# Inner sums of x ahead of the sixth out product's additions in VectorE's order (last two units of a RetNet + SwiGLU kernel)

## The chip, the cores and the metric

The kernel runs on one core of a Trainium2 chip. The core's engines are TensorE (PE in the profile, PEld for its weight loads), VectorE (DVE), ScalarE (ACT), GpSimd (POOL) and SyncE (SP, which issues the DMAs). The metric is the device time of one execution in microseconds; lower is better.

## The reference, cut to what matters

The program computes a retention layer and then a gated feed-forward network, all in float32:

```python
scores = q @ k^T / 8                      # (8 batches, 8 heads, 576, 576), head dimension 64
x = (scores * decay) @ v                  # -> x of 4608 tokens x 512
xn = x / sqrt(mean(x * x) + 1e-6) * rms_g
g, val = xn @ w_gate, xn @ w_val          # 512 -> 1536 each
out = (g * sigmoid(g) * val) @ w_out      # 1536 -> 512
```

The change lies in the second part, between the end of one block of tokens and the start of the next.

## The kernel before, in words

**Units.** The 4608 tokens are worked in nine units of 512 (u = 0 to 8). x of a unit is held transposed, as four chunks of 128 features by 512 tokens. Units 0 and 1 and the retention of the early batches are worked in a written-out plan; the loop at the end of the program does u = 2 to 8. Each pass of it has an up phase (`up` or `up_deep`, six pieces n = 0 to 5, which alternate between gate and value) and an out phase (`across`).

**Fewer products.** Both phases use a 2 x 2 block scheme of seven products in place of eight (Strassen's, in Winograd's form), which needs sums and differences of the blocks before the products and additions of the products behind them. In the out phase and in the deep stages the scheme is applied twice, one inside the other: seven outer products of seven inner ones. The blocks are called A11, A12, S1, A22, S2, S3, S4.

**Deep stages.** For the last two units (LATE: u = 7 and 8) the first four up pieces (DEEP: n = 0 to 3) are done by `up_deep`. Each has seven outer products in the order A11, S2, S1, S3, A12, S4, A22; each outer product is seven inner ones (line 884, 128 x 128 by 128 x 128, two matmul instructions each, 14 in all), which write two PSUM banks: xo and xp, then yo and yp, zo and zp, wo and wp, then xo/xp, zo/zp and wo/wp again. VectorE adds them up (line 905) and ScalarE copies some (line 901). GpSimd then combines the results (line 913), and ScalarE (gate, SiLU, line 925) or VectorE (value, product, line 923) makes h of them one stage later.

**The moving operands of a deep stage.** Three of the seven inner products of an outer product take a plain quarter of an operand; the other four need inner sums. `inner_x` (lines 837 to 857) makes them ahead of the unit, once for all four stages, in two parts:

- part 0 fills the tile inner_x from x itself, for the blocks A11, S1, A12 and S4: four additions of 128 x 512;
- part 1 fills the tile deep_x (deep_x2 in the code) from the tile sums, for the blocks S2, S3 and A22: four additions of 128 x 384.

In each part the first two additions are independent of each other; the third needs the second, and the fourth the third. The first deep product (A11) needs part 0 alone. The second (S2) needs part 1: first its three plain inner products are worked (yo twice, yp once), then the four with deep_x.

**The out phase.** `across(u)` is a generator. It makes its operands and then works seven outer products n = 0 to 6 (line 1090) into the banks of x, z, x, z, y, w, x. Each product has an early and a late half, and the generator yields after each half, so that the caller can put other work between them: yield 0 comes before the first product, yield 2n + 1 after the early half of product n and yield 2n + 2 after its late half and the additions that follow it. What follows the last three products is:

- n = 4 (banks yo, yp): two additions each into two of the four blocks of vec (the tile vi), and one addition of 128 x 896 (line 1113);
- n = 5 (banks wo, wp), the sixth product: `add(3, 3, "w")` and `add(1, 1, "w")`, four VectorE operations (line 1117: wo 128 x 512 and wp 128 x 384, each twice);
- n = 6 (banks xo, xp), the seventh: `add(1, 1, "x")`, two operations.

Behind them GpSimd combines vec (`combine`, line 1286). GpSimd also makes the inner sums of the out operands ahead of their products (lines 1042 and 1047).

**Between the two.** The loop behind `across(u)` puts the preparation of unit u + 1 at yields of `across(u)`: its norm at yield 2, the scaling of x at 3 to 6, the sums of x (the tile sums, line 626) at 8, and, where u + 1 is 7 or 8, `inner_x` at the yields that the table XI_AT names: part 0 at yield 11, part 1 at yield 12.

**What sets the order.** The whole program is under `tc.manual_schedule()`: each engine works its instructions in the order in which the code issues them, and waits on semaphores where data or a buffer is not ready. So VectorE's order around the end of `across(u)` is: additions of n = 4, part 0, the four additions of n = 5, part 1, the two additions of n = 6, then the additions of the first deep stage.

**PSUM banks.** All of PSUM is one pool of eight banks; a new tile gets a bank that an earlier one has left. In units 7 and 8 the program places the first deep stage's banks so: x on those that the out phase's y left, y on those of z, z (zo, zp) on those of w (wo, wp), and w on those of x. So the third deep product, z, can write only when `add(1, 1, "w")` has read the banks of the sixth out product.

**Weights.** They stream from DRAM into one large tile (ring) by SyncE's DMAs, each issued when TensorE has used the piece whose place it takes.

Of the kernel before, what the change touches and what calls it, by code (L numbers as in the profile page):

```python
# [44 lines left out]
def kernel(  # L45
# [11 lines left out]
    nc = tc.nc  # L57
# [200 lines left out]
    def prepare(j):  # L258

        d = st[j]  # L260
        for odd in range(2):
            t = d["qraw"][:, odd::2]
            nc.scalar.activation(
                out=t, in_=t, func=AF.Copy, scale=gp[:, jobs[j][1], odd : odd + 1]
            )
        for nm in ("q", "k"):
            t = att.tile([P, S], F32, tag=nm + "T", name=f"{nm}T_{j}")
            nc.vector.transpose(out=t, in_=d.pop(nm + "raw").rearrange("p t a -> p (t a)"))
            d[nm + "T"] = t
        scale_v(j)  # L270
# [364 lines left out]
    LATE = (NU - 2, NU - 1)  # L635
# [172 lines left out]
    def inner_blocks(u, n):  # L808


        i = pieces.index(("up", u, n))
        assert n_used <= i < n_sent
        a, z = places[i]
        w = ring[:, a:z].rearrange("p (b x) -> p b x", b=7)
        d = w_in_d[n - DEEP[0]]
        t6 = vi[:, NV : NV + 6 * 4 * P].rearrange("p (b s f) -> p b s f", b=6, s=4)
        t1_ = row(f"inner_{n}").rearrange("p (b s f) -> p b s f", b=1, s=4)
        for t, b in ((t6, slice(0, 6)), (t1_, slice(6, 7))):
            a11, a21, a12, a22 = (w[:, b, i * P : i * P + P] for i in range(4))
            s1, s2, s3, s4 = (t[:, :, i] for i in range(4))  # L820
            for o, x, y, op in (
                (s3, a11, a21, ALU.subtract), (s1, a21, a22, ALU.add),
                (s2, s1, a11, ALU.subtract), (s4, a12, s2, ALU.subtract),
            ):
                nc.gpsimd.tensor_tensor(out=o, in0=x, in1=y, op=op)

        def save(i):
            b = PLACE[IN_ORDER[i]]
            t = t6[:, b] if b < 6 else t1_[:, 0]
            nc.sync.dma_start(  # L830
                out=d[:, i * 4 * P : i * 4 * P + 4 * P], in_=t.rearrange("p s f -> p (s f)")
            )

        saves.extend(lambda i=i: save(i) for i in range(7))

    def inner_x(u, part, eng):


        if not deep_x1:
            retention.close()  # L840
            late = ctx.enter_context(tc.tile_pool(name="late", bufs=1))
            deep_c.extend(late.tile([P, 4, 7, P], F32, name=f"deep_c_{i}") for i in range(2))
            deep_x2.append(late.tile([P, 4, 3, P], F32, name="deep_x2"))
            deep_x1.append(
                xp.tile([P, NHP, U], F32, tag="x", name="inner_x")
                .rearrange("p k (a t h) -> p k a t h", a=2, t=2)
            )
        x = x_of[u].rearrange("p (a c) (t s h) -> p c s a t h", c=2, t=2, s=2)
        y = sums_x.rearrange("p i c (s h) -> p c s i h", s=2)
        for o, v_ in (((deep_x1[0], x), (deep_x2[0], y))[part],):  # L850
            t1_, t3, t2, t4 = (o[:, i] for i in range(4))
            x11, x12, x21, x22 = v_[:, 0, 0], v_[:, 0, 1], v_[:, 1, 0], v_[:, 1, 1]
            for r, a, b, op in (
                (t1_, x12, x11, ALU.subtract), (t3, x22, x12, ALU.subtract),
                (t2, t3, x11, ALU.add), (t4, x21, t2, ALU.subtract),
            ):
                eng.tensor_tensor(out=r, in0=a, in1=b, op=op)  # L857

    def up_deep(u, n):

# [174 lines left out]
    def inner_sums(u, n, part=None, eng=nc.gpsimd):  # L1035

        x = operands_of(u)[order_of(u)[n]]
        x11, x12 = x[:, :NK, :P], x[:, :NK, P:]
        x21, x22 = x[:, NK:, :P], x[:, NK:, P:]
        i1, i3, i2, i4 = inner_of(u, n)  # L1040
        if part != 1:
            eng.tensor_tensor(out=i1, in0=x12, in1=x11, op=ALU.subtract)  # L1042
        c = slice(1, NK) if part == 1 else slice(0, 1) if part == 0 else slice(0, NK)
        for o, a, b, op in (
            (i3, x22, x12, ALU.subtract), (i2, i3, x11, ALU.add), (i4, x21, i2, ALU.subtract),
        ):
            eng.tensor_tensor(out=o[:, c], in0=a[:, c], in1=b[:, c], op=op)  # L1047
# [231 lines left out]
    def combine(b, eng=nc.vector, late=False):  # L1279

        t = vec[:, b] if isinstance(b, slice) else vec[:, b : b + 1]
        for o, x, y in (
            (A12, A11, A12), (A11, A11, S2), (S1, A11, S1), (S4, S1, S4), (A11, A11, S3),
            (S3, S1, S3), (A22, A11, A22),
        ):
            eng.tensor_tensor(out=t[:, :, o], in0=t[:, :, x], in1=t[:, :, y], op=ALU.add)  # L1286
        if late:
            store(NU - 1, b)
# [3 lines left out]
    def store(u, b=None):  # L1292

        rows = out[u * U : u * U + U].rearrange("(C c p) (R r x) -> c r p C R x", C=2, c=2, R=2, r=2)
        v4 = vec.rearrange("p (C R) n d -> p C R n d", C=2)
        for n, (r, c) in CORNERS.items():
            if b is None:
                for half in range(2):
                    nc.sync.dma_start(out=rows[c][r][:, half], in_=v4[:, half, :, n])
            else:  # L1300
                nc.sync.dma_start(out=rows[c][r][:, b // 2, b % 2], in_=vec[:, b, n])
# [252 lines left out]


    z = DEEP[-1]
    XI_AT = {11: (0, nc.vector), 12: (1, nc.vector)}
    FINISH = {(z + 1, 5): 1, (z + 1, 6): 1, (z + 2, 1): 1} if z % 2 else {(z + 1, 1): 3, (z + 1, 4): 2}
    with tc.manual_schedule():
        start()  # L1560
        for u in range(2, NU):
            j0 = NHP * (u + 1)
            more = u + 1 < B
            for n in range(2 * NG):
                deep = u in LATE and n in DEEP
                for i, _ in enumerate((up_deep if deep else up)(u, n)):
                    if u in MAKES:
                        if (n, i) == ((0, 0) if MAKES[u] < 4 else (1, 3)):
                            inner_blocks(u, MAKES[u])
                        if (n, i) == (0, 0):  # L1570
                            combine(slice(0, 4), nc.gpsimd)
                    if saves and (n, i) >= (0, 4):
                        saves.pop(0)()
                    if (n, i) == ((2 * NG - 1, 0) if u in MAKES else (1 + (u in LATE), 4)):
                        store(u - 1)
                    if (n, i) == ((2 * NG - 1, 2) if u in LATE else (2 * NG - 2, 1)):
                        inner_sums(u, 0, 0)
                        inner_sums(u, 1, 0)
                    if more and i == 2 and 0 < n <= NHP:
                        if j0 + n < len(jobs):  # L1580
                            prepare(j0 + n)
                            fetch(j0 + n + 1)
                    if u + 1 < NU and n == 2 * NG - 1:
                        if i < NHP:
                            gather(u + 1, i, square(u + 1, i))
                        elif i == NHP:
                            fold(u + 1)
                        elif i == 6:
                            meet(u + 1)
                    if (u, n, i) == (2, 2, 1):  # L1590
                        same_rows()
                    for _ in range(FINISH.get((n, i), 0) if u in LATE else 0):
                        unfinished.pop(0)()
                    if more and (n, i) == (NHP, 5) and j0 + NHP == len(jobs):
                        values(j0 + NHP - 1)
                if more and n <= NHP and (n or u == 2):
                    if j0 + n < len(jobs):
                        slot(j0 + n, rest=(n > 0))
                    else:
                        carried(j0 + n - 1)  # L1600
            assert not unfinished and not saves
            for i, _ in enumerate(across(u)):
                if u + 1 == NU:
                    continue
                if i == 2:
                    root(u + 1)
                elif i in (3, 4, 5, 6):
                    scale_x(u + 1, (i - 3,))
                elif i == 8:
                    sums_of_x(u + 1)  # L1610
                if i in XI_AT and u + 1 in LATE:
                    inner_x(u + 1, *XI_AT[i])


# [25 lines left out]
```

## Time and profile before

| | |
|---|---|
| timed runs | median 1093.52 us of 3 (1093.32 to 1093.53) |
| profiled execution | 1092.14 us, of which the span of the profile is 1090.3 us |
| TensorE busy | 1076.3 us, 99% of the span |
| VectorE busy | 763.6 us, 70% |
| GpSimd busy | 556.5 us, 51% |
| ScalarE busy | 337.0 us, 31% |
| granted TensorE clock | 0.998 of full speed |
| operations of part 1 (128 x 384) | 0.55 to 0.56 us each |
| operations of part 0 (128 x 512) | 0.69 us, three of eight 1.48 us |
| additions of the sixth product (line 1117) | 0.68 us (wo) and 0.55 us (wp) |

The times of single instructions come from the profiled execution, which is taken once; the median comes from runs without a profile. A stretch of the program is found in the timeline by its lines and tiles: the out phase of unit 6 ends and unit 7 begins at about 881 us, the out phase of unit 7 ends and unit 8 begins at about 983 us. Operations on one engine overlap at their edges: an operation can start before the one ahead of it has ended.

### The profile page before, as it was taken

To read this page: it belongs to the slowest core of one execution; us is meant where nothing else is said; L and a number is where in the kernel's file an instruction comes from. 1 tells how busy PE (TensorE), PEld (TensorE's weight loads), DVE (VectorE), ACT (ScalarE), POOL (GpSimd) and SP (SyncE) were. 2 spreads that over 40 slices of the span, in tenths; PEclk is the share of its full clock that TensorE was granted. 3 is DMA by queue.
4 is the path that set the end of the run, shared out by engine and by line. 5 is a ranking of instruction groups with operands and counts; after the bars stand their busy time and mean duration, and the time that the engine had idled before them with its cause. 6 is when DMAs were issued, how large, how long until landed. Compare 5 with 4: busy or idle time off the path is not lost. (4 is left out here: it accounts for less than half of the span.)

```text
span 1090.3 us, 25380 instructions
## 1 busy us (share of the span) xinstructions
PE 1076.3 (99%) x10342; PEld 913.9 (84%) x10342; DVE 763.6 (70%) x1355; ACT 337.0 (31%) x763; POOL 556.5 (51%) x509
## 2 busy tenths in 40 slices
PE   8899999999999999999999999999999999999998
PEld 6754444479988899889988998889888999899998
DVE  3878568877876775667667765777465877686677
ACT  5855564331123411332034202331233112212210
POOL 0026326538530288126652476229601968896876
PEclk9999999999999999999999999999999999999999
DMA  8856798697978976898779975889676889499951
GB/s 205 195 174 243 290 244 211 213 336 196 286 284 227 197 275 237 225 231 269 271 223 209 275 288 186 248 207 366 220 195 207 274 288 342 177 308 351 331 204 40
DMA packets 271860, 265.68 MB, mean 244 GB/s; under 512 B 194304, under 2 KB 214912, under 8 KB 266624
## 3 DMA queue, kind: packets, MB, share of 16 engines
q1 hardware_dynamic: 270304, 263.67, 77.7%
q8 instruction: 81, 1.33, 0.5%
q10 hardware_dynamic: 1440, 0.40, 0.2%
q14 instruction: 35, 0.29, 0.1%
HBM read 226.61 MB, written 37.42 MB: 242 GB/s over the span
## 5 line engine op out<-in xcount | busy, mean ns | idle before, releaser
L980 PE MATMUL up<-x,ring 128*128 128x512 f32 x384 | 167.1, 594 | 0.0
L980 PEld LDWEIGHTS up<-x,ring 128*128 128x128 f32 x384 | 72.2, 190 | 89.3 <-issue 84.9
L746 PE MATMUL x<-x,ring 128*128 128x256 f32 x544 | 130.8, 383 | 0.0
L746 PE MATMUL w<-sums,ring 128*128 128x256 f32 x544 | 128.6, 379 | 0.0
L746 PE MATMUL z<-x,ring 128*128 128x256 f32 x544 | 128.5, 379 | 0.0
L1042 POOL TENSOR_TENSOR vi<-h 128x384 f32<-128x384 f32 x32 | 41.7, 1304 | 161.4 <-DVE h L765 148.9
L746 PEld LDWEIGHTS z<-x,ring 128*128 128x128 f32 x544 | 103.4, 190 | 14.1
L746 PEld LDWEIGHTS w<-sums,ring 128*128 128x128 f32 x544 | 103.2, 190 | 14.2
L746 PEld LDWEIGHTS x<-x,ring 128*128 128x128 f32 x544 | 101.0, 190 | 14.2 <-ACT m L772 0.2
L1047 POOL TENSOR_TENSOR vi<-h 128x384 f32<-128x384 f32 (+2 forms) x46 | 45.6, 991 | 116.6 <-DVE h L765 116.6
L1286 POOL TENSOR_TENSOR vi<-vi 128x512 f32<-128x512 f32 (+1 forms) x77 | 79.5, 1045 | 36.3 <-DVE vi L1117 19.8
L913 POOL TENSOR_TENSOR deep_c<-deep_c 128x512 f32<-128x512 f32 x56 | 73.1, 1317 | 11.4 <-DVE deep_c L905 5.1
L746 PE MATMUL y<-sums,ring 128*128 128x256 f32 x272 | 64.3, 379 | 0.0
L753 DVE TENSOR_TENSOR h<-u,w 128x512 f32<-128x512 f32 x34 | 23.4, 687 | 49.8 <-PE w L746 49.8
L746 PEld LDWEIGHTS y<-sums,ring 128*128 128x128 f32 x272 | 51.7, 190 | 7.0
L1406 POOL TENSOR_TENSOR vi<-vi 128x512 f32<-128x512 f32 (+1 forms) x24 | 40.7, 1696 | 30.3 <-DVE vi L1395 16.9
L1406 POOL TENSOR_TENSOR ring<-ring 128x512 f32<-128x512 f32 x24 | 30.4, 1272 | 49.7 <-DMA w_up_blocks<-ring 24.8
L753 DVE TENSOR_TENSOR u<-m,y 128x512 f32<-128x512 f32 x34 | 23.3, 685 | 44.0 <-PE y L746 37.7
L767 ACT ACTIVATE h<-h 128x512 f32<-128x512 f32 x51 | 32.0, 629 | 62.6 <-DVE h L753 62.6
L334 DVE SCALAR_TENSOR_TENSOR ret<-s,causal 128x256 f32<-128x256 f32 (+2 forms) x112 | 32.0, 337 | 21.8 <-PE s L296 21.8
L1047 POOL TENSOR_TENSOR vi<-h,vi 128x384 f32<-128x384 f32 (+2 forms) x46 | 45.5, 988 | 3.6
L772 ACT COPY m<-x 128x512 f32<-128x512 f32 x34 | 19.9, 585 | 86.8 <-PE x L746 86.8
(386 smaller groups left out, 2416.8 us busy)
## 6 DMA issues: line engine op xcount, KB each, us to landing
ring<-w_out_blocks SPq DMA_DIRECT2D x59, 1344.0 KB, 7.0
ring<-w_up_blocks SPq DMA_DIRECT2D x34, 1792.0 KB, 8.9
w_out_blocks<-vi SPq DMA_DIRECT2D x21, 448.0 KB, 6.2
out_dram<-vi SPq DMA_DIRECT2D x64, 128.0 KB, 6.0
ring<-w_in_blocks SPq DMA_DIRECT2D x8, 1024.0 KB, 6.8
qraw<-in_q_dram SPq DMA_DIRECT2D x96, 72.0 KB, 5.2
kraw<-in_k_dram SPq DMA_DIRECT2D x96, 72.0 KB, 3.3
k<-in_k_dram SPq DMA_DIRECT2D x48, 128.0 KB, 3.3
```

The costliest lines, as they stand in the source:

```text
L334: nc.vector.scalar_tensor_tensor(out=ret[:p, e, a:z], in0=s[e][:p, a * L : z * L].rearrange("p (c k) -> p c k", k=L), scalar=float(_gamma( ...
L746: nc.tensor.matmul(ps[:, i * HU : i * HU + HU], lhsT=w[:, PLACE[blk], c, i * P : i * P + P], rhs=t_of[u][blk][:, c], start=(start and i == ...
L753: nc.vector.tensor_tensor(out=o, in0=a, in1=pairs_of(ps), op=ALU.add)
L767: nc.scalar.activation(out=o, in_=c, func=AF.Silu)
L772: nc.scalar.copy(out=s1, in_=pairs_of(x_))
L913: nc.gpsimd.tensor_tensor(out=c[:, which, at(o)], in0=c[:, which, at(x)], in1=c[:, which, at(y)], op=ALU.add,)
L980: nc.tensor.matmul(ps, lhsT=w[:, PLACE[blk], c % 2, i * P : i * P + P], rhs=x_of[u][:, c], start=(c == 0), stop=(c == NHP - 1),)
L1042: eng.tensor_tensor(out=i1, in0=x12, in1=x11, op=ALU.subtract)
L1047: eng.tensor_tensor(out=o[:, c], in0=a[:, c], in1=b[:, c], op=op)
L1286: eng.tensor_tensor(out=t[:, :, o], in0=t[:, :, x], in1=t[:, :, y], op=ALU.add)
L1406: nc.gpsimd.tensor_tensor(out=t[o], in0=t[x], in1=t[y], op=op)
```

## The change

At yield 11 both parts of `inner_x` are issued, and none at yield 12. In VectorE's order the four operations of part 1 so stand directly behind those of part 0 and ahead of the four additions of the sixth out product. This happens twice in the program, in `across(6)` for unit 7 and in `across(7)` for unit 8. The table XI_AT and the engine argument of `inner_x` go; the engine was VectorE for both parts and stays it.

```diff
-    def inner_x(u, part, eng):
+    def inner_x(u, part):
...
-                eng.tensor_tensor(out=r, in0=a, in1=b, op=op)
+                nc.vector.tensor_tensor(out=r, in0=a, in1=b, op=op)
...
-    XI_AT = {11: (0, nc.vector), 12: (1, nc.vector)}
...
-                if i in XI_AT and u + 1 in LATE:
-                    inner_x(u + 1, *XI_AT[i])
+                if i == 11 and u + 1 in LATE:
+                    inner_x(u + 1, 0)
+                    inner_x(u + 1, 1)
```

## The prediction

> **What bounds the kernel now.** I read the page first: TensorE is busy almost throughout, so time can only be won where it stands still.
>
> ```profile
> span 1090.3 us, 25380 instructions
> PE 1076.3 (99%) x10342; PEld 913.9 (84%) x10342; DVE 763.6 (70%) x1355; ACT 337.0 (31%) x763; POOL 556.5 (51%) x509
> ```
>
> Then the waits of TensorE and of its weight loads from 880 us on (line waited for: us in total, times, longest):
>
> ```profile
> PE yo L884 <- DVE deep_x L857: 1.7, 2, 1.2
> PEld yo L884 <- DVE deep_x L857: 2.1, 2, 1.4
> ```
>
> Two waits, one per deep unit, both for the four operations that the diff moves (deep_x is the second tile of inner_x). Then the timeline of the second place (start, length, engine and line, out<-in, and in brackets the idle time before it and its releaser):
>
> ```profile
> 981.91 0.69 DVE L857 TENSOR_TENSOR inner_x<-x,inner_x 128x512 f32<-128x512 f32 x1
> 982.52 0.68 DVE L1117 TENSOR_TENSOR vi<-vi,wo 128x512 f32<-128x512 f32 x1
> ...
> 983.58 0.68 DVE L1117 TENSOR_TENSOR vi<-vi,wo 128x512 f32<-128x512 f32 x1
> ...
> 984.18 0.55 DVE L1117 TENSOR_TENSOR vi<-vi,wp 128x384 f32<-128x384 f32 x1
> ...
> 984.65 1.02 DVE L857 TENSOR_TENSOR deep_x<-sums 128x384 f32<-128x384 f32 x2
> ...
> 984.88 0.61 PE L884 MATMUL yo<-sums,ring 128*128 128x128 f32 x4
> ...
> 986.29 0.56 DVE L857 TENSOR_TENSOR deep_x<-sums,deep_x 128x384 f32<-128x384 f32 x1
> 986.77 0.68 DVE L1117 TENSOR_TENSOR vi<-vi,xo 128x512 f32<-128x512 f32 x1
> ...
> 986.91 0.71 PE L884 MATMUL yo<-deep_x,ring 128*128 128x128 f32 x4 [1.19 <-DVE deep_x L857]
> ...
> 987.90 0.61 PE L884 MATMUL zo<-x,ring 128*128 128x128 f32 x4
> ```
>
> The reader sees VectorE without a pause: the additions of the sixth out product (wo, wp), then deep_x, then the additions of the seventh (xo). TensorE starts its second deep product (yo) at 984.88, runs out of ready operands, and goes on at 986.91, when deep_x is done. At unit 7 the same rows stand at 879.85 (first wo addition), 881.98 (deep_x), 884.10 (xo addition), and for TensorE 882.90 (yo) and 885.23 (zo).
>
> **The size of the two stalls.** A deep product is 14 matmul instructions; without a wait it takes 1.56 us from start to start (unit 7: xo 881.34, yo 882.90; later zo 885.23, wo 886.80). From yo to zo it took 885.23 - 882.90 = 2.33 us in unit 7 and 987.90 - 984.88 = 3.02 in unit 8: 0.77 and 1.46 too long, **2.23 us** in all. The waits view gives 1.69 (0.50 + 1.19) on TensorE, since the modelled end of the matmul in front covers part of it. I take start to start, and keep 1.69 as the other end.
>
> **The change part by part.** Nothing is added or removed: eight VectorE operations at each of two places change their order, no DMA and no other queue is touched. In VectorE's queue the wo/wp group (982.52 to 984.65, 2.13 us; 879.85 to 881.98, 2.13) and the deep_x group (984.65 to 986.77, 2.12; 881.98 to 884.10, 2.12) change places. What is behind both, the xo/xp additions and all that follows, keeps its time.
>
> deep_x, earlier: it starts at 982.52 and its last operation ends 2.20 us on (986.29 + 0.56 - 984.65), at 984.72. TensorE needs it six instructions after 984.88, at 985.55: 0.83 us spare. Unit 7: 882.05 against 883.57. Both stalls go: **-0.77 and -1.46**. deep_x reads only sums, done before 975, so it has nothing else to wait for.
>
> wo/wp additions, later: two things wait for them. GpSimd's combining additions (L1286) also need the xo/xp additions, which don't move, so they start when they do now (987.53). The PSUM banks are the other: the next unit's third product z writes banks 3 and 4, which are those of wo and wp. The third addition of the group frees wo, the fourth wp. Moved by 2.12, unit 8's end at 983.58 + 0.68 + 2.12 = 986.38 and 984.18 + 0.55 + 2.12 = 986.85. The weight load of zo, now at 987.79, would come at 987.79 - 1.46 = 986.33; a release takes about 0.05 here (deep_x ended at 986.85, the load began at 986.90), so it starts at 986.43: 0.10 late. zp's load, now 988.24, comes at 986.88 and is released at 986.90: 0.02 more. Unit 7: released 883.76 and 884.23, wanted 884.35 and 884.80: no wait. So **+0.12**. Bounds: nothing, if the group ends 0.1 sooner, and 0.21 by the nearest row, a wait met equally narrowly: in the fourth deep stage of unit 7 zo started at 922.85 behind a VectorE addition that ended at 922.80, and wo came at 924.53 where 921.19 + 2 x 1.565 is 924.32. I take 0.12.
>
> What is late next: the w product needs the xo bank, freed at 987.45 as now; its first matmul, now at 989.46, would come at 988.12: 0.67 spare. Weights land at least 9.9 us before the matmul that needs them in both units, so an earlier TensorE finds them there.
>
> Whether the gain lasts: GpSimd's queue starts at a fixed time and runs full, 987.53 to 996.65, then the sums of the first deep stage 996.77 to 1005.90. Its next work started at 1007.71 after 1.82 us idle. The profile names a SiLU (L925) as the releaser, but that work needs VectorE's last addition of the second stage, which ended at 1007.57; it will come 1.34 sooner, at 1006.37, still 0.47 after 1005.90 (unit 7: 904.27 against 903.23). So GpSimd follows TensorE again from there. ScalarE's SiLUs stay and delay one VectorE addition by 0.4 us (1009.61 could be 1008.27, the copy it needs ends at 1008.58), which 1.9 us until its next operand absorb. From there to the last matmuls every stage hangs on TensorE, and the tail behind 1071 us moves as a whole.
>
> **A rule against the change.** The inner sums take 1.48 us or 0.68 for one 128x512 operation: three of the four inner_x<-x in the trace ran beside GpSimd's inner sums (until 877.34 and 980.60) and took 1.48; one started behind them and took 0.68. The wo additions, with one input in PSUM, took 0.68 throughout. The Trainium skill (SBUF — State Buffer, section Who interferes with whom) says that a VectorE instruction with two SBUF inputs contends with a GpSimd instruction that reads SBUF, and one with at most one such input does not. By that rule the change brings an exposed group 2.13 us closer to GpSimd's work in place of a safe one; it would cost if GpSimd were still at work, and by the rows above it is not, so by rule and rows together the sum stays.
>
> **Sum.** -0.77 - 1.46 + 0.12 = -2.11 us. Against the profiled execution (1092.14, span 1090.3) that is 1090.0. The three timed runs lie higher, median 1093.52; the same difference gives **1091.4**. What a measurement of this kernel can tell from no change is about 0.2%, 2.19 us: the forecast lies just inside.
>
> **Rivals.**
> 1. The z banks cost more: if the moved additions end later than worked out, unit 8 pays at once (unit 7 after 0.6 us). With 0.5 us more: gain 1.6, 1091.9; the stall sum of 1.69 gives the same (1.57). For it: no spare in unit 8. Against: the rows of both units agree within 0.02 us.
> 2. Given back later: were GpSimd's 1007.71 start really bound to the SiLUs, the combined values for VectorE's products (L923 at 1016.87) would stay where they are. VectorE is full from there to the fourth stage's z product (1025.51), where TensorE already waits 0.2 us; that wait would grow by up to 0.77 and 1.34. Gain 0 to 1: 1092.5 to 1093.5. Against: the two spares, 1.04 and 0.47.
> 3. The order on VectorE doesn't change, or another operand ends the same wait: 1093.5. Against: the rows stand in the order of the code, and deep_x is named as releaser with nothing behind it.
> 4. Slower: GpSimd's inner sums reach into the moved group. Four operations stretched like inner_x (1.48 for 0.68, times 0.55: 1.20, +0.65 each) end 2.6 us later; zo's load then comes at 986.43 + 2.6 = 989.0 against 987.79 now, and at 886.36 against 885.12 in unit 7: +2.5, 1096.0. It begins once GpSimd works past 879.85 and 982.52, where the moved groups will start, and costs all of this once it works to their ends; now it ends 2.51 and 1.92 us ahead of these starts.
>
> **How the numbers follow.** Forecast (gain 1.8 to 2.4) 0.73, rival 1 0.12, rival 2 0.07, rival 3 0.03, rival 4 0.05. Since 2.11 is so close to 2.19, the forecast's 0.73 is split by the bounds of the bank wait and of the stalls: 0.36 beyond 0.2%, 0.37 within. Faster 0.36; same 0.37 + 0.12 + 0.07 + 0.03 = 0.59; slower 0.05. The range, 1090.6 to 1093.1, takes in a forecast with no bank wait and some drift of the base (0.2 us between the runs shown), rival 1 and the better part of rival 2.
>
> **What would show it.** Right: no wait of yo for deep_x; the VectorE operations in the new order; yo to zo 1.56 us in unit 7 and about 1.7 in unit 8, there with a wait of zo for vi (L1117); span near 1088.2. Wrong: a zo wait over 0.5 us, an L857 operation of 128x384 over 0.6 us, or the fourth stage's zo wait grown beyond 0.2.

## The result, and the profile after

In 17 timed runs of each kernel the changed kernel took 1091.79 us (median; 1088.63 to 1093.62), the kernel before 1093.53 us (1090.98 to 1096.68). The ratio is **0.9978**, 95% interval 0.9968 to 0.9987: about 2.4 us faster, at least 1.4 and at most 3.5. (The means of the runs differ by 2.45 us, the medians by 1.74; single runs of one kernel lie up to 5.7 apart.)

The profiled execution of the changed kernel says the opposite at first sight: its span is 1091.0 us, where that of before was 1090.3.

```profile
span 1091.0 us, 25384 instructions
PE 1077.1 (99%) x10342; PEld 914.7 (84%) x10342; DVE 763.1 (70%) x1355; ACT 337.1 (31%) x763; POOL 557.5 (51%) x509
```

The time was lost far ahead of the change, where both kernels are the same, and most of it at the start of the program. The windows view gives, for the first 60 us, the length, the busy time of each engine with its instructions in brackets, the granted clock, the share of the DMA engines and GB/s; first the kernel before, then the changed one:

```profile
0.00:60.00 60.00, 53.18 (x1313) 41.90 (x1314) 37.51 (x106) 38.83 (x100) 2.42 (x15) 0.97 0.82 203
```

```profile
0.00:60.00 60.00, 52.40 (x1268) 41.75 (x1268) 36.46 (x102) 37.81 (x97) 2.72 (x14) 0.94 0.83 204
```

In the same 60 us TensorE got through 1313 instructions before and 1268 after. Unit 7's first deep matmul came at 881.34 us before and at 884.07 after, 2.73 us later. Of this, 1.8 us had been lost by 57 us (the same matmul of line 980 starts at 55.01 and at 56.79), and 0.9 in one step later (line 407 at 720.85 and at 723.56, where it waits for ScalarE); the first operation that the diff moves starts at 882.57. From there on the changed kernel gains. At unit 8 (timeline, as in the prediction):

```profile
984.52 1.02 DVE L857 TENSOR_TENSOR deep_x<-sums 128x384 f32<-128x384 f32 x2
...
986.17 0.56 DVE L857 TENSOR_TENSOR deep_x<-sums,deep_x 128x384 f32<-128x384 f32 x1
...
986.65 0.68 DVE L1117 TENSOR_TENSOR vi<-vi,wo 128x512 f32<-128x512 f32 x1
...
986.86 0.61 PE L884 MATMUL yo<-sums,ring 128*128 128x128 f32 x4
...
987.53 0.61 PE L884 MATMUL yo<-deep_x,ring 128*128 128x128 f32 x4
987.71 0.68 DVE L1117 TENSOR_TENSOR vi<-vi,wo 128x512 f32<-128x512 f32 x1
...
988.31 0.55 DVE L1117 TENSOR_TENSOR vi<-vi,wp 128x384 f32<-128x384 f32 x1
988.51 0.52 PEld L884 LDWEIGHTS zo<-x,ring 128*128 128x128 f32 x4
988.54 0.68 PE L884 MATMUL zo<-x,ring 128*128 128x128 f32 x4
...
988.95 0.30 PEld L884 LDWEIGHTS zp<-x,ring 128*128 128x128 f32 x2
```

deep_x is done at 986.73 and TensorE takes it at 987.53 without a pause: 0.67 us behind the start of yo, which is six instructions. From yo to zo it takes 1.57 us in unit 7 and 1.68 in unit 8, where it took 2.33 and 3.02. The wait for deep_x is gone from the waits view. Instead there is the narrow wait of the prediction, of zo for the bank wo. Without a wait zo would start 1.56 us behind yo, at 988.42, and its weight load 0.11 ahead of that, at 988.31. The load comes at 988.51, 0.20 late, behind the second wo addition (987.71 + 0.68 = 988.39). The load of zp follows it at its usual distance (0.44 us) and waits for nothing more. The waits view has no row for this wait; only the start times show it.

**A measure that leaves the start out.** From unit 7's first deep matmul (line 884) to the start of the last matmul of the program it is 1085.65 - 881.34 = 204.31 us before and 1086.37 - 884.07 = **202.30** after: 2.01 us. Behind the last matmul both have about the same tail, 4.67 and 4.61 us. This stretch is what the experiments are compared by. Where an expectation names a stretch to the end of the span, that is the same with the tail (208.98 and 206.91).

### The profile page after: what moved, and what is told of

Same layout as the page of the kernel before. It is cut to its first block, busy times and chain, and to the rows that moved or that the text cites. A ratio compares the mean times of both kernels' runs of the same rounds, so it can differ in the third digit from the quotient of the medians.

```text
span 1091.0 us, 25384 instructions
## 1 busy us (share of the span) xinstructions
PE 1077.1 (99%) x10342; PEld 914.7 (84%) x10342; DVE 763.1 (70%) x1355; ACT 337.1 (31%) x763; POOL 557.5 (51%) x509
## 4 chain that ended last, share of the span: by engine, by line
PE 95%; DVE 1%; DMA 1%; issue 1%; SPq 0%; ACT 0%; POOL 0%; POOLq 0%; DVEq 0%; ACTq 0%
PE up L980 15%; PE x L746 11%; PE w L746 11%; PE z L746 11%; PE xo L1090 6%; PE y L746 5%; PE xp L1090 4%; PE zo L1090 4%; PE zp L1090 3%; PE wo L1090 2%; PE yo L1090 2%; PE av L387 2%; PE wp L1090 2%; PE s L296 2%; PE av L407 2%; PE yp L1090 2%
## 5 line engine op out<-in xcount | busy, mean ns | idle before, releaser
L1286 POOL TENSOR_TENSOR vi<-vi 128x512 f32<-128x512 f32 (+1 forms) x77 | 80.1, 1054 | 36.3 <-DVE vi L1117 19.8
```

## Experiments

Each was profiled once; the one with two more edits was also timed several times, against the kernel before. Where each took its time, in us:

| kernel | yo to zo, unit 7 | yo to zo, unit 8 | first deep to last matmul |
|---|---|---|---|
| before | 2.33 | 3.02 | 204.31 |
| before again | 2.30 | 3.06 | 204.33 |
| changed | 1.57 | 1.68 | 202.30 |
| changed again | 1.57 | 1.67 | 202.30 |
| change for unit 8 alone | 2.32 | 1.66 | 203.02 |
| part 1 last | 8.06 | 8.74 | 217.63 |
| part 1 beside GpSimd | 1.57 | 1.57 | 205.72 |
| changed, wo first | 1.57 | 1.57 | 202.27 |
| changed, GpSimd + 1 | 1.57 | 1.66 | 203.13 |
| changed, GpSimd + 2 | 1.57 | 1.66 | 205.76 |
| changed, two more edits | 1.57 | 1.57 | 201.80 |
| before, part 1 + 2 | 3.51 | 4.21 | 208.32 |
| before, part 1 + 6 | 6.74 | 7.48 | 217.06 |

The theory is that of the prediction: the gain is the two pauses of yo, made there and kept to the end, less a narrow wait of zo. Its rivals are chance of the single execution, another cause of the pauses, and a give-back through GpSimd (time won here and lost again later).

**Both kernels once more.**

> The kernel before once more, for the measure of all runs here: the time from the first deep matmul of unit 7 (line 884, xo) to the end of the span, which leaves out everything ahead of the change. It was 1090.32 - 881.34 = 208.98 us in the kernel before and 1090.98 - 884.07 = 206.91 in the changed one. Theory (the gain is the two stalls of yo, made there and kept to the end): 208.9 to 209.1 again, yo to zo 2.33 us in unit 7 and 3.02 in unit 8, whatever the span. Rival (the time moves with something of the single execution, such as the start of the program or the transfers): this stretch varies like the spans do, by a microsecond or more.

> The changed kernel once more. Theory: 206.8 to 207.0 us from the first deep matmul of unit 7 to the end of the span, yo to zo 1.57 us in unit 7 and 1.7 in unit 8, whatever the span. Rival (chance of the execution): anything within a microsecond or two of 207.9, the mean of both kernels.

The spans were 1092.1 and 1088.0 us, so now 4.1 us apart the other way; the stretch is 204.33 and 202.30 against 204.31 and 202.30. The measure repeats within 0.02 us, and what lies ahead of unit 7 carries the variation: over the profiles here, unit 7 begins anywhere from 880.9 to 885.5 us. Chance of the execution is out as the cause of the 2.01 us.

**The change for unit 8 alone.**

```diff
                 if i == 11 and u + 1 in LATE:
                     inner_x(u + 1, 0)
-                    inner_x(u + 1, 1)
+                if i == (11 if u + 1 == NU - 1 else 12) and u + 1 in LATE:
+                    inner_x(u + 1, 1)
```

> The change for unit 8 alone; unit 7 keeps the order of the kernel before. Theory (two stalls, each worth its own length): unit 7 stalls as before (yo to zo 2.33), unit 8 has yo to zo 1.57 or 1.7, with the narrow wait of zo for the moved additions; stretch 208.98 - 1.28 = 207.7. Rival (what is won in unit 7 sets the gain, or the second stall depends on the first): the stretch stays at 209.0 or falls to 206.9.

203.02, 1.29 us under the kernel before; unit 7 paused as before. To the span's end it was 207.69 where 207.7 was expected. The two pauses are independent, and the other unit's 0.72 makes up the whole.

**Part 1 last.**

```diff
-                    inner_x(u + 1, 1)
+                if i == 14 and u + 1 in LATE:
+                    inner_x(u + 1, 1)
```

> Part 1 behind the additions of the seventh out product too (yield 14), 1.15 us later than in the kernel before (two operations, 986.77 to 987.92). Theory (TensorE follows deep_x one for one): each stall grows by 1.15, yo to zo 3.5 and 4.2 us, stretch 208.98 + 2.3 = 211.3; GpSimd's combining additions, which wait for the seventh product's additions, start 2.1 us earlier and win nothing. Rival (deep_x is only named by the profile, the wait is for something else, for instance the banks): no change, 209.0; or, if the earlier combining additions matter, less than 209.

The direction was right and the size far off: the stretch is 217.63, 13.3 us more than before, not 2.3. Instructions that write deep_x (count, then shortest, median and longest in ns), GpSimd's combining beside them at unit 8, and the windows of unit 8 (columns as above):

```profile
L857 DVE TENSOR_TENSOR deep_x<-sums x4: 1370/1497/1612, 884.4 to 995.0; 128x384 f32<-128x384 f32 x4
L857 DVE TENSOR_TENSOR deep_x<-deep_x,sums x2: 1500/1501/1502, 887.3 to 996.7; 128x384 f32<-128x384 f32 x2
```

```profile
993.42 9.99 POOL L1286 TENSOR_TENSOR vi<-vi 128x512 f32<-128x512 f32 x7 [4.80 <-DVE vi L1117]
```

```profile
993.00:994.00 1.00, 0.72 (x7) 0.52 (x5) 1.00 (x3) 0.66 (x2) 0.58 (x1) 1.00 1.01 367
...
995.00:996.00 1.00, 0.00 (x0) 0.00 (x0) 1.00 (x2) 0.00 (x0) 1.00 (x1) 1.00 1.02 348
996.00:997.00 1.00, 0.00 (x0) 0.00 (x0) 0.97 (x2) 0.00 (x0) 0.92 (x2) 0.82 1.02 395
997.00:998.00 1.00, 0.00 (x0) 0.00 (x0) 1.00 (x1) 0.00 (x0) 0.92 (x2) 0.50 0.54 207
...
1002.00:1003.00 1.00, 1.00 (x7) 1.00 (x6) 0.49 (x1) 0.00 (x0) 1.00 (x2) 0.50 0.00 0
1003.00:1004.00 1.00, 1.00 (x9) 1.00 (x9) 0.17 (x1) 0.00 (x0) 0.41 (x1) 0.76 0.00 0
```

The expectation had left out two prices. It had named the earlier start of GpSimd's combining (L1286), which the seventh product's additions release, but not that part 1 then runs beside it: each operation took about 1.5 us in place of 0.56, from the first start to the last end 5.97 us (993.73 to 998.20 + 1.50) in place of 2.20, 3.77 more. And in TensorE's pause of 6.0 us its granted clock fell to 0.50, from 996.6 to 1003.5 us, so the next matmuls took twice as long. For unit 8 this gives 1.15 + 3.77 for deep_x and about 1.7 for the clock (0.8 within yo to zo, 0.9 behind zo): 6.6. Unit 7 paid 6.7 in the same way, together 13.3.

**Before, part 1 + 2 and + 6.** To lengthen the pauses without GpSimd at work beside part 1, the kernel before got repetitions of part 1's first operation:

```diff
-                eng.tensor_tensor(out=r, in0=a, in1=b, op=op)
+                for _ in range(3 if part == 1 and r is t1_ else 1):      # 7 in the second run
+                    eng.tensor_tensor(out=r, in0=a, in1=b, op=op)
```

> The kernel before with the first operation of part 1 done two more times in front of itself (the same values). It moves deep_x later by about 2 x 0.48 = 0.96 us and nothing ahead of it, with no GpSimd work beside it, which the run with part 1 last did not manage. Theory (TensorE follows deep_x one for one): yo to zo 2.33 + 0.96 = 3.3 us in unit 7 and 4.0 in unit 8, first deep matmul to last matmul 204.31 + 1.9 = 206.2. Rival (something else ends the wait): no change, 204.3, or only a part.

> The same with six more, about 2.9 us. Theory (one for one, and a pause of this length still leaves the granted clock at full speed): yo to zo 5.2 and 5.9 us, first deep matmul to last matmul 204.31 + 5.8 = 210.1, clock 1.0 throughout both units. Rival (the longer pause of TensorE, about 3.4 us in unit 7 and 4.1 in unit 8, already brings the half clock that the 6 us pause with part 1 last brought): up to 1.7 us more in each unit in which the clock falls, 211.8 to 213.5.

A repetition cost 0.59 us and not 0.48: that is the distance at which part 1's dependent operations follow each other (985.70 to 986.29 in the kernel before). With two, unit 7's yo to zo grew by 1.18 and unit 8's by 1.19: one for one, so deep_x is the cause of the pauses and nothing else ends them later. But the stretch grew by 4.01, not 2.37: behind unit 8's pause the clock fell. PE's rows of unit 7 and then unit 8 (the code stands one line lower here), and the windows of unit 8:

```profile
886.02 0.71 PE L885 MATMUL yo<-deep_x,ring 128*128 128x128 f32 x4 [1.68 <-DVE deep_x L858]
```

```profile
989.89 0.71 PE L885 MATMUL yo<-deep_x,ring 128*128 128x128 f32 x4 [2.38 <-DVE deep_x L858]
...
991.82 1.06 PE L885 MATMUL zo<-inner_x,ring 128*128 128x128 f32 x4
```

```profile
990.00:991.00 1.00, 1.00 (x10) 1.00 (x11) 1.00 (x3) 0.00 (x0) 0.49 (x1) 1.00 1.05 406
991.00:992.00 1.00, 1.00 (x8) 1.00 (x7) 0.96 (x2) 0.00 (x0) 0.92 (x2) 0.62 0.50 191
992.00:993.00 1.00, 1.00 (x7) 1.00 (x6) 0.08 (x1) 0.00 (x0) 1.00 (x1) 0.50 0.00 0
```

Unit 7's pause (1.68 us by the row, 3.51 - 1.56 = 1.95 start to start) left the clock at full speed; unit 8's (2.38 and 2.65) was followed, from 991.2 to 994.7 us, by half of it, which cost 1.08 us from zo to wo and 0.55 in the product behind. With six repetitions both units' pauses (4.0 and 4.8 by the rows) brought half clock for 6.8 us each: 12.75 us in all, of which 2 x 3.54 are the repetitions and the rest, 5.7, the clock. The expectation of a clock at full speed failed, and so did the rival's bound of 1.7 a unit (it was 2.8).

Length alone does not sort these pauses. In all 13 traces every change of the granted clock stands a whole multiple of 3.41 us behind the trace's first clock record; in the run with two repetitions 885.43 and 991.24 us are such points. Unit 7's pause (884.34 to 886.02) lay across one of them, with 1.09 us on one side and 0.59 on the other. Unit 8's (987.51 to 989.89) had 2.05 us in the one stretch that ended at 991.24, where the clock fell. From unit 7's first deep matmul to the last matmul, over all traces, the stretches of 3.41 us with up to 1.55 us free of matmuls kept the clock, and the five with 2.05 us or more were followed by half of it; between the two nothing was measured. The kernel before, with pauses of 0.77 and 1.46, kept the clock.

**Part 1 beside GpSimd.**

```diff
+                if i == 9 and u + 1 in LATE:
+                    inner_x(u + 1, 1)
                 if i == 11 and u + 1 in LATE:
                     inner_x(u + 1, 0)
-                    inner_x(u + 1, 1)
```

> Part 1 at yield 9, directly behind the sums of x and ahead of the fifth product's additions, so beside GpSimd's inner sums; part 0 stays at yield 11. Theory (the rule on the shared port holds for this form too: two SBUF inputs beside GpSimd): the first two 128x384 operations take about 1.2 us each in place of 0.55, part 0 then starts about 2.1 to 3.4 us later than now and meets less of GpSimd. If the additions of the fifth and sixth product stay in time (xo of the first deep stage writes the banks of the fifth product, needed from 884 us on) the stretch stays near that of the changed kernel, 206.9, with a wait of xo for inner_x of up to 1 us in place of the spare there: 206.9 to 208.5. Rival (the rule does not bite on 128x384): operations of 0.55 us, stretch 206.9.

```profile
977.41 2.51 DVE L857 TENSOR_TENSOR deep_x<-sums 128x384 f32<-128x384 f32 x2
979.96 1.24 DVE L857 TENSOR_TENSOR deep_x<-deep_x,sums 128x384 f32<-128x384 f32 x1
981.23 1.24 DVE L857 TENSOR_TENSOR deep_x<-sums,deep_x 128x384 f32<-128x384 f32 x1
...
985.63 1.29 DVE L857 TENSOR_TENSOR inner_x<-x 128x512 f32<-128x512 f32 x2
```

The price of one operation beside GpSimd was right (1.24 us against 1.2 expected), but all four paid it, and the wait of xo for inner_x was 1.8 us in each unit where up to 1 was expected: the stretch is 205.72, 3.4 us more than in the changed kernel. Part 0, moved out of GpSimd's way, took 0.68 to 0.69 us throughout. Two of GpSimd's operations beside part 1 went from 1.00 to 1.31 us. So the rule of the prediction agrees with this form too, and here both engines paid.

**The narrow wait: wo first.**

```diff
-                add(3, 3, "w")
-                add(1, 1, "w")
+                for half in range(2):
+                    for b in (3, 1):
+                        o, ps = parts(vec[:, b], "w")[half]
+                        nc.vector.tensor_tensor(out=o, in0=o, in1=ps, op=ALU.add)
```

> The changed kernel with the sixth product's four additions in the order wo, wo, wp, wp in place of wo, wp, wo, wp. Theory (the 0.18 us that unit 8 still loses between yo and zo is the wait for wo's bank, freed by the second wo addition): that addition ends about 0.45 us sooner, zo comes without a wait; zp may wait up to 0.1. yo to wo in unit 8 falls from 3.31 to between 3.13 and 3.25 us, the stretch from 206.91 to about 206.8. Rival (the 0.18 is something else): 3.31 again.

zo came without a wait (yo to zo 1.57), but zp then waited for wp: zo to wo 1.70 us in place of 1.64. yo to wo fell from 3.31 to 3.26, just outside the expected 3.13 to 3.25: about 0.05 of 0.19 us is saved. That zo waited for wo's bank is shown by its start; that the stretch fell to 202.27 is at the edge of the measure (to the span's end, with the tail, the time even grew).

**The give-back: GpSimd + 1 and + 2.** The changed kernel with a multiplication by ones, 128x512, ahead of the first deep stage's combining:

```diff
         def combine_in(which):
             at = PARTS.index
+            for _ in range(1 if n == 0 else 0):                           # 2 in the second run
+                part = c[:, which, at(A12)]
+                one = ones.unsqueeze(1).to_broadcast([P, 4, P])
+                nc.gpsimd.tensor_tensor(out=part, in0=part, in1=one, op=ALU.mult)
```

> The changed kernel with one more GpSimd operation (a multiplication by ones, 128x512, about 1.3 us) ahead of the combining of the first deep stage, in both units; the values stay the same. Theory of the give-back (GpSimd's queue has 1.20 us to spare in unit 7 and 0.68 in unit 8 before its second stage; what goes beyond reaches VectorE's products and the fourth stage's wait of zo): 0.1 + 0.6, stretch 206.91 + 0.7 = 207.6. Rival (VectorE or ScalarE absorb it): 206.9.

> The same with two operations, about 2.6 us. Theory of the give-back: 1.4 us beyond the spare in unit 7 and 1.9 in unit 8, so the fourth stage's zo waits that much more than the 0.2 it waits now; stretch 206.91 + 3.3 = 210.2. Rival (absorbed): 206.9; half-way, if a part of it is absorbed.

+0.83 and +3.46 us, where 0.7 and 3.3 were expected; in the first deep stage nothing changed, and the time went where the second rival had put it, to the fourth stage. GpSimd's rows of the changed kernel at unit 8, then VectorE's row and TensorE's wait with two operations:

```profile
989.53 9.13 POOL L1286 TENSOR_TENSOR vi<-vi 128x512 f32<-128x512 f32 x7 [6.92 <-DVE vi L1117]
998.61 9.13 POOL L913 TENSOR_TENSOR deep_c<-deep_c 128x512 f32<-128x512 f32 x7
1008.42 9.14 POOL L913 TENSOR_TENSOR deep_c<-deep_c 128x512 f32<-128x512 f32 x7 [0.68 <-ACT h L925]
```

```profile
1020.88 1.29 DVE L927 TENSOR_TENSOR h<-h,deep_c 128x512 f32<-128x512 f32 x2 [1.94 <-POOL deep_c L917]
```

```profile
PEld zo L884 <- DVE deep_c L905: 3.7, 2, 2.1
```

GpSimd had 0.68 us to spare in unit 8, where it had 1.82 before the change (and 1.20 against 1.81 in unit 7). One operation of 1.3 us uses that up and costs 0.67 more there and 0.17 in unit 7, two cost 2.0 and 1.5. So the path of the give-back is real, and the change stopped 0.68 us short of it. In the second profile of the changed kernel the work behind this idle time (1005.47, idle 0.65) is put down to VectorE's last addition of the second stage (deep_c, L905) and not to a SiLU, as the prediction had read it.

**Two more edits.** Besides wo first, the two differences of the fourth deep stage (line 1004) behind that stage's w additions:

```diff
         add(first, first, "y")
-        if m:
+        if m and n != DEEP[-1]:
             finish(len(unfinished) - 4)
...
         add(c[:, C22], c[:, C22], "w")
+        if m and n == DEEP[-1]:
+            finish(len(unfinished) - 4)
         yield
```

> The changed kernel with two more edits in VectorE's order: the sixth product's additions as wo, wo, wp, wp, and in the fourth deep stage the two differences (line 1004, 2.3 us) behind that stage's w additions in place of ahead of its z additions. Theory (what TensorE still waits in these two units is queue order on VectorE: 0.21 us at the fourth stage's zo and zp in each unit, and 0.1 to 0.2 in unit 8's first stage): the waits in the fourth stage go, yo to zo to wo of unit 8's first stage as in the kernel with wo first. From the first deep matmul of unit 7 to the last matmul 202.30 - 0.42 - 0.03 = 201.85 us (the kernel before: 204.31); in the timed runs 2.5 us under the kernel before, ratio about 0.9977, against the changed kernel not to be told apart. Rival (the differences are needed where they stand): a new wait behind them, stretch 202.3 or more.

```profile
1025.74 0.61 PE L884 MATMUL xo<-x,ring 128*128 128x128 f32 x4
...
1027.30 0.61 PE L884 MATMUL zo<-x,ring 128*128 128x128 f32 x4
```

In unit 8's fourth stage, shown here, xo to zo is 1.56 us, where the changed kernel took 1.67. No deep product of unit 7 waits any more, and in unit 8 only zp of the first stage does (zo to wo 1.70). The stretch is 201.80 against 201.85 expected, 2.51 us under the kernel before. Timed: ratio 0.9977 to the kernel before (interval 0.9967 to 0.9987). The trace tells it from the changed kernel by 0.5 us; the timed runs (0.9977 here, 0.9978 for the changed kernel) do not.

## Why the prediction was right

- **The size of the stalls**: 0.77 and 1.46 by start to start were right; the changed kernel and the change for unit 8 alone won them, and 1.69 by the idle times would have been too little. The repetitions in the kernel before show the cause: one for one.
- **deep_x earlier**: predicted 0.83 us to spare in unit 8; it was done at 986.73 and taken at 987.53, 0.80 (0.69 by the weight load of that matmul, at 987.42).
- **The narrow wait of zo**: predicted 0.12, measured 0.19 from yo to wo, inside the bound of 0.21; none in unit 7, as predicted. The term was too small because zo's load was 0.20 us late, not 0.10: the addition ended 0.08 behind the time at which the load was due, not 0.05, and the load came 0.12 behind the addition, not 0.05. The 0.02 more for zp did not arise, since its load was held up no further. What the load lost shows as 0.12 from yo to zo and 0.07 from zo to wo.
- **The sum**: -2.11 predicted, -2.01 in the stretch, 2.4 (1.4 to 3.5) in the timed runs. The median fell by 1.74, to 1091.79, where 1091.4 was forecast. With single runs up to 5.7 us apart, that the medians agree so closely is in part luck; the stretch is the better test. The prediction had split its chances at 0.2%: the interval, 0.13 to 0.32%, tells the change from none, but not on which side of 0.2% it lies.
- **Rival 1** (z banks): they cost 0.07 us more than the 0.12 predicted, not 0.5 more. **Rival 2** (give-back): its path exists and its sizes hold, but it begins 0.68 us further on; the prediction had put the spare at 0.47 and 1.04, measured 0.68 and 1.20. **Rival 3**: VectorE's rows stand in the new order. **Rival 4** (GpSimd beside the moved group): the price of one operation, 1.20, was borne out with 1.24 and 1.50, but GpSimd's sums ended ahead of the group and it paid nothing (0.55 and 0.56).
- **What failed**: "span near 1088.2" as a sign. One profile gave 1091.0 and another 1088.0, because what lies ahead of unit 7 varies by more than the change is worth. The wait of zo for vi, another sign, is there by the start times and by the run with wo first, but not in the waits view. The fourth stage's zo wait stayed at 0.2 us, as said.
- **The rule** of the Trainium skill (SBUF — State Buffer, section Who interferes with whom) agrees with these runs: additions with one input in PSUM took 0.68 us beside GpSimd and without it, those with both in SBUF 1.24 to 1.50 in place of 0.55. The prediction was right to weigh it by where GpSimd stood; the runs with part 1 beside GpSimd and with part 1 last show what a move of a few microseconds more would have cost.

## What to carry to other kernels

Two groups in one queue can change places for nothing when the slack of the group moved back is more than the time of the group moved forward and the stall that goes, together. Here the additions had 3.5 us until their banks were written again. The inner sums took 2.1 and the stall 0.8 in unit 7, which fits, and 1.5 in unit 8, which just fails to; so all but 0.2 of 2.2 us was won. Size a short stall by start to start of the instructions around it, not by the idle time shown, and measure a change of 0.2% from an event ahead of it to an event behind it: the span of one execution moved the wrong way. Before moving work that an idle engine is waiting for further back, look what else the work in front of it releases.

## What the runs showed of the hardware that was not expected

- TensorE's granted clock fell to 0.50 after a pause of 2.65 us start to start (2.38 by the row), for 3.4 us, which cost 1.6 us. A pause of 1.95 (1.68 by the row) left it at full speed, and pauses of 4.0 to 6.0 us by the rows brought 6.8 us of half clock. The changes stand on a grid of 3.41 us, and the fall goes with how much of a pause lies within one step of it (1.55 us and less kept the clock, 2.05 and more did not). The Trainium skill (TensorE: Matmul & The Clock Gate, section Why this matters for your kernels) advises against gaps of over about 3 us; here the fall came at a shorter one. So a stall of some 2 to 3 us can cost more than itself.
- What lies ahead of unit 7 moved it by 4.6 us from profile to profile (880.9 to 885.5), and up to 3.1 us of that had arisen in the first 60 us. The granted clock of the first 60 us does not order them: it was 0.94 where unit 7 began at 884.1 (changed) and where it began at 880.9 (change for unit 8 alone). What moves it stays open; no run was made for it.
